# An issue order from a list schedule whose urgencies are shifted by fixed seeds

## The chip, the cores and the metric

The kernel runs on one core of a Trainium2 chip. The metric is device time in microseconds of one execution; the median of several runs counts, and less is better. The engines are called by the profile's short names: PE is TensorE's matmuls and PEld its weight loads, DVE is VectorE, ACT is ScalarE, POOL is GpSimd, SP is SyncE, which issues most transfers.

## The reference

Two branches work on one input of 2048 rows and 512 columns, and a gate mixes them. The first branch builds a convolution kernel of length 2048 for each of the 512 channels from a sum over 128 complex modes, convolves the input with it through Fourier transforms, and adds a skip term. The second is linear attention with 32 heads, whose feature map is a softmax of a small projection and of its negative.

```python
def reference(A_u, A_A_re, A_A_im, ..., B_wqkv, B_w_phi, B_wo, gate_w):
    x = A_u
    g = sigmoid((x * gate_w).sum(-1, keepdims=True))
    # first branch
    logdA = dt * (A_re + 1j * A_im); dB = dt * Bc          # dt = exp(log_dt)
    P = exp(logdA[:, :, None] * l[None, None, :])          # l = 0 .. 2047
    K = einsum("dn,dnl,dn->dl", Cc, P, dB).real
    a = irfft(rfft(pad(u)) * rfft(pad(K)))[..., :L] + u * Dskip
    # second branch, head width 16
    q, k, v = split(x @ wqkv)
    phi(t) = concat(softmax(t @ w_phi), softmax(-(t @ w_phi)))
    b = (phi(q) @ (phi(k).T @ v)) / (phi(q) @ sum(phi(k)) + 1e-6) @ wo
    return g * a + (1 - g) * b
```

## The kernel before

The work is first written down as a plan and only then issued. Each call of `P.add` enters one piece: the engine that does it (or a choice of ACT and DVE for some PSUM evictions), its cost in microseconds, the function that issues its instructions, the pieces that it waits for, and the buffers that it takes and drops. A piece is one to some dozens of instructions. `P.dma` enters a transfer as its issue on SP and its landing. When everything is entered, `Plan.run` puts the pieces into one order, by a list schedule over the plan's own times, and then calls their functions in that order. Each engine thus gets a fixed queue, and on the chip each queue is worked off strictly in order.

The list schedule repeats one step. Of all pieces whose predecessors are placed, and which find their buffer and (on ACT) the right table set, it takes the one that can start earliest in the plan's time. Among pieces with the same start it takes the one with the highest urgency (`n.prio`), which is the sum of costs on the longest chain of pieces behind it, with 0.2 us for each change of engine. A piece that waits for a busy engine starts when the engine comes free, so equal starts are frequent. `boost` adds to the urgency but is set to 0.0 everywhere.

Rings limit the order. `ps` has two PSUM slots that serve every stage; `p0` has two that serve the start, `bk` three for keys and queries, and `pf` two that open when the queries are done. In SBUF, A and R have two buffers each, KD one, Eq (`r8`) two, E and cs four each. A piece that takes a slot waits for the piece that drops it.

The stages, in the order of their entry:

- `prepare`: constants, trigonometric tables, the tables C and D of the modes, the transposed input xT.
- `keys_and_spectrum`: the input's spectrum XU, then the gate, then keys and values for eight pairs of row blocks. The gate is five pieces: 64 small products `gps`, a clip, an exponential, a reciprocal (into `gT`), and a second product `zps` with the eviction into `at.zrow`.
- `queries_and_convolution`, first the queries: four batches, each with four products pq and their exponentials into Eq, a normaliser in steps z1 to z5 (ACT, DVE, ACT, DVE, ACT; the last makes `apm`), and for each of four row blocks two products aexp, two DVE products into Eq, and one block of 12 matmuls into bps (eight with Mw and Eq, four for the skip term). z2 reads `at.zrow`.
- The convolution for eight halves h of 64 channels: `plan_tables` makes E (exponentials) and cs (sines) from `args` products, and switches ACT to the sine tables and back; its two args tiles for the sines hold both PSUM slots that they took until the sines are made. `kgen` makes, for two chunks, A (two halves of three DVE products, L1065 to L1067) and R (L1077 to L1080), then the product kps (64 small matmuls, L241), its eviction KD (L1098), two products psA (L1110) and their evictions XA. `transform` goes on with psB, XK, the spectral products t, psz, a round trip through DRAM (Zd, ZT), psy and the output bS.

The A and R products of the first halves may run during the queries. From half 2 on, the psA products wait for `sq`, the piece that closes the queries, frees their buffers and opens `pf`. Half h + 2's tables are entered after half h's kgen.

Of the kernel before, what the change touches and what calls it, by code (L numbers as in the profile page):

```python
# [91 lines left out]
class Plan:  # L92


    LAT = 0.2

    def __init__(self, rings, psum):
        self.k, self.dyn, self.nodes = dict(rings, **psum), set(psum), []
        self.boost = 0.0
        self.keys, self.shut = {}, {"bk", "pf"}  # L100

    def add(self, eng, cost, fn, deps=(), take=(), drop=(), late=0.0, rw=("", ""), tab=None, sets=None, opens=None):
        n = Bag()
        n.eng, n.cost, n.fn, n.take, n.drop, n.late = eng, cost, fn, list(take), list(drop), late
        n.tab, n.sets, n.opens, n.ring = tab, sets, opens, None
        n.deps = [d for d in deps if d is not None]
        for k in rw[0].split() + rw[1].split():
            wr, rd = self.keys.setdefault(k, (None, []))
            n.deps += ([wr] if wr is not None else []) + (rd if k in rw[1].split() else [])
        for k in rw[0].split():  # L110
            self.keys[k][1].append(n)
        for k in rw[1].split():
            self.keys[k] = (n, [])
        n.users, n.t, n.i, n.boost = [], None, len(self.nodes), self.boost
        n.psum = None
        if "psum" in n.drop:
            n.psum = [d for d in n.deps if d.dyn][0]
        n.dyn = any(not isinstance(r, str) or r in self.dyn for r in n.take)
        for d in n.deps:
            d.users.append(n)  # L120
        self.nodes.append(n)
        return n
# [11 lines left out]
            self.keys[k] = (n, [])  # L134
        return n

    def run(self):
        self.nodes = list(self.nodes)

        for r, k in self.k.items():  # L140
            if r in self.dyn:
                continue
            tk = [n for n in self.nodes for x in n.take if x == r]
            dr = [n for n in self.nodes for x in n.drop if x == r]
            for j, n in enumerate(tk):
                for d in ([dr[j - k]] if j >= k else []) + ([tk[j - 1]] if j and tk[j - 1] is not n else []):
                    assert d.i < n.i
                    n.deps.append(d)
                    d.users.append(n)
        for n in reversed(self.nodes):  # L150
            n.prio = n.boost + n.cost + max([u.prio - u.boost + self.LAT * (u.eng != n.eng) for u in n.users], default=0.0)
        free = {}
        taken = {r: 0 for r in self.k}
        given = {r: {} for r in self.k}
        left = list(self.nodes)
        state, since = None, {}
        order = []
        while left:
            best = None
            for n in left:  # L160
                if any(d.t is None for d in n.deps):
                    continue
                best_e = None
                for e, c in (n.eng if isinstance(n.eng, list) else [(n.eng, n.cost)]):
                    t = free.get(e, 0.0) if e not in "WX" else 0.0
                    for d in n.deps:
                        t = max(t, d.end + (self.LAT if d.at != e else 0.0))
                    if best_e is None or t + c < best_e[0]:
                        best_e = (t + c, t, e, c)
                _, t, e, c = best_e  # L170
                if n.tab is not None and n.tab != state:
                    continue
                ok, ring = True, None
                for r in n.take:
                    if isinstance(r, str) and r not in self.dyn:
                        continue
                    alt = []
                    for q in ([r] if isinstance(r, str) else r):
                        m = taken[q] - self.k[q]
                        if q in self.shut or (m >= 0 and m not in given[q]):  # L180
                            continue
                        alt.append((max(t, given[q][m] + self.LAT if m >= 0 else since.get(q, 0.0)), -self.k[q] + taken[q], q))
# [4 lines left out]
                if not ok:  # L187
                    continue
                key = (t, -n.prio, n.i)
                if best is None or key < best[0]:  # L190
                    best = (key, n, e, c, ring)
            assert best is not None, "no piece can start"
            (t, _, _), n, e, c, ring = best
            n.t, n.end, n.at = t, t + c, e
            free[e] = n.end
            if ring is not None:
                n.ring, n.slot = ring, taken[ring]
                taken[ring] += 1
            if n.psum is not None:
                k = n.psum  # L200
                given[k.ring][k.slot] = n.end
            if n.sets is not None:
                state = n.sets
            if n.opens is not None:
                self.shut.discard(n.opens)
                since[n.opens] = n.end
                self.shut.add({"bk": "p0", "pf": "bk"}[n.opens])
            left.remove(n)
            order.append(n)
        order.sort(key=lambda n: (n.t, n.i))  # L210
        self.order = order
        for n in order:
            self.cur = n
            n.fn()
        return max(n.end for n in order)


def build_selectors(nc, persist, tp, icol):

# [386 lines left out]
def keys_and_spectrum(P, tc, nc, g, psum):  # L606
# [23 lines left out]
    for h in range(2):  # L630
        X = Bag()
        en = []
        for g4 in range(gw // 4):
# [15 lines left out]
            a = P.add("PE", 1.0, pa, [a] if g4 else last, take=[("ps", "p0") if h == 0 else "ps"] + (["XAu"] if g4 == 0 else []), rw=("ud0 ud1 ud2 ud3 W1", ""))  # L649
            en.append(evict(ea, [a]))  # L650
        for r0 in range(0, 32, 4):
# [11 lines left out]
            a = P.add("PE", 0.75, pb, en + [a], take=[("ps", "p0") if h == 0 else "ps"], rw=("TB0 TB1 TB2", ""), drop=(["XAu"] if r0 == 28 else []))  # L663
# [5 lines left out]
    for h in range(2):  # L669
# [15 lines left out]
        a = P.add("PE", 1.2, fa, last + ([a] if h else []), take=["ps"] + ([] if h else ["XAu"]), rw=("wqk ic", ""))  # L685
        fn.append(evict(fe, [a]))
    for h in range(2):
# [16 lines left out]
        a = P.add("PE", 1.2, fb, fn + [a, at_n], take=["ps"], drop=(["XAu"] if h else []))  # L704
# [29 lines left out]
    a = P.add("PE", 1.8, ga, xt + [at_n], take=["ps"])  # L734
    b = P.add("DVE", 0.2, gb, [a], drop=["psum"])
    b = P.add("ACT", 0.2, lambda: act(out=G.z[:], in_=G.z[:], func=ACT.Exp, scale=-1.0), [b, lnexp], tab="L")
    P.add("DVE", 0.4, gc, [b])

    def gd():
        G.ps = psum([128, 4, 128], "zps")  # L740
# [7 lines left out]
        nc.vector.tensor_scalar(out=at.zrow[:], in0=G.ps[:], scalar1=80.0, scalar2=-80.0, op0=ALU.min, op1=ALU.max)  # L748
        G.ps = None
    a = P.add("PE", 1.1, gd, [b, sp], take=["ps"])  # L750
    P.add("DVE", 0.6, ge, [a], drop=["psum"])

    kv = []
    for s2 in range(8):
        K = Bag()
        red = []
        for u in range(2):
# [20 lines left out]
            a = P.add("PE", 1.05, pk, [a] if u else [sp, lnexp] + xt + kp, take=["bk"] + ([] if u else ["Ek", "Zk", "vr"]))  # L778
            x = P.add("ACT", 1.22, ex, [a] + ([x] if u else []), drop=["psum"], tab="L")
# [8 lines left out]
        for u in range(2):  # L788
# [25 lines left out]
            a = P.add("PE", 1.05, pv, [a], take=["bk"], rw=("wqk", ""))  # L814
            c = P.add("DVE", 1.36, sc, [a, l], drop=["psum"])
# [54 lines left out]
def queries_and_convolution(P, tc, nc, g, psum, sh, sp, sl, kv, bank, evict):  # L870
# [36 lines left out]
    a = P.add("PE", 0.9, f2, [n1], take=[psq])  # L907
    n3 = evict(f3, [a])
    mw = []
    for i in range(0, 8, 2):  # L910
# [11 lines left out]
        a = P.add("PE", 0.55, f4, [n3, a], take=[psq])  # L922
# [4 lines left out]
        g.shift_keys()  # L927
    sk = P.add("X", 0.0, shift_k, mw + [sl])

    P.boost = 0.0  # L930
    qdone = []
    for b in range(4):
        Q = Bag()
        eq = []
        for m in range(4):
# [14 lines left out]
            a = P.add("PE", 1.0, pq, [sh, sp] + ([a] if m else []), take=["bk"] + ([] if m else ["r8"]))  # L950
# [35 lines left out]
            act(out=Q.apm[:], in_=Q.lnZ[:], func=ACT.Exp, scale=-1.0)  # L986
            Q.lnZ = Q.den = None
        n = P.add("ACT", 0.8, z1, [z], tab="L")
        n = P.add("DVE", 1.0, z2, [n], drop=["acc"])
        n = P.add("ACT", 0.35, z3, [n], tab="L")  # L990
        n = P.add("DVE", 0.4, z4, [n])
        za = P.add("ACT", 0.35, z5, [n], tab="L")
        pb = None
        for i in range(4):
            j = 4 * b + i
            em = []
            for mp in range(2):
# [12 lines left out]
                a = P.add("PE", 0.3, pe, [za], take=["bk"])  # L1010
# [30 lines left out]
    P.boost = 0.0  # L1041

    xan = [0, 0]

# [261 lines left out]
    T, prev = {}, []  # L1306
# [25 lines left out]
def full_kernel(tc, A_u, A_A_re, A_A_im, A_B_re, A_B_im, A_C_re, A_C_im, A_log_dt, A_Dskip,  # L1332
# [7 lines left out]
    with ExitStack() as ctx:  # L1340
# [181 lines left out]
```

## Time and profile before

| what | value |
|---|---|
| median of 3 runs | 359.31 us (357.62 to 360.52) |
| profiled execution | 359.8 us, its span 358.0 us |
| mean granted TensorE clock | 0.80 of full speed |
| busy share of the span | DVE 79%, PE 71%, ACT 71%, PEld 42%, POOL 3% |
| data moved | 24.62 MB, 69 GB/s over the span |

The profiled execution is one run on the chip; its span goes from the first to the last instruction. A busy share is an average over the whole span, so it says little about any one stage. [...]

### The profile page before, as it was taken

To read this page: it belongs to the slowest core of one execution; us is meant where nothing else is said; L and a number is where in the kernel's file an instruction comes from. 1 tells how busy PE (TensorE), PEld (TensorE's weight loads), DVE (VectorE), ACT (ScalarE), POOL (GpSimd) and SP (SyncE) were. 2 spreads that over 40 slices of the span, in tenths; PEclk is the share of its full clock that TensorE was granted. 3 is DMA by queue.
4 is the path that set the end of the run, shared out by engine and by line. 5 is a ranking of instruction groups with operands and counts; after the bars stand their busy time and mean duration, and the time that the engine had idled before them with its cause. 6 is when DMAs were issued, how large, how long until landed. Compare 5 with 4: busy or idle time off the path is not lost.

```text
span 358.0 us, 9785 instructions
## 1 busy us (share of the span) xinstructions
PE 255.8 (71%) x4291; PEld 150.7 (42%) x4320; DVE 283.8 (79%) x482; ACT 254.7 (71%) x328; POOL 10.3 (3%) x24
## 2 busy tenths in 40 slices
PE   0235684769998895798999769669586847985850
PEld 0234563664444352353455424435244522554640
DVE  8959999986999978999547872169989998697521
ACT  2397999867757689838875692769899897985400
POOL 7200010000000000000000000000000000000000
PEclk9985667657999999598999967757857986585995
DMA  7993400000000000011021001631515264689354
GB/s 202 204 110 75 103 3 0 2 2 0 4 3 2 2 2 2 0 23 37 19 46 31 16 15 29 134 135 55 127 56 122 90 148 146 131 197 207 112 95 66
DMA packets 58665, 24.62 MB, mean 69 GB/s; under 512 B 54144, under 2 KB 55296, under 8 KB 58112
## 3 DMA queue, kind: packets, MB, share of 16 engines
q1 hardware_dynamic: 54400, 23.10, 29.0%
q10 hardware_dynamic: 4224, 0.92, 1.2%
q8 instruction: 33, 0.54, 0.6%
q14 instruction: 8, 0.07, 0.1%
HBM read 11.42 MB, written 8.39 MB: 55 GB/s over the span
## 4 chain that ended last, share of the span: by engine, by line
DVE 42%; PE 33%; ACT 11%; issue 7%; DMA 4%; SPq 1%; DVEq 0%; ACTq 0%
PE bps L1018 7%; DVE A L1065 4%; DVE Atmp L1066 4%; PE pq L943 4%; DVE A L1067 4%; DVE Zk L776 4%; DVE vr L800 3%; PE kps L241 3%; DVE R L1080 2%; PE aexp L1003 2%; ACT cs L83 2%; ACT L75 2%; DMA wqk<-in_B_wqkv_dram 2%; DVE pt L454 2%; DVE R L1079 2%
## 5 line engine op out<-in xcount | busy, mean ns | idle before, releaser
L1018 PE MATMUL bps<-Mw,Eq 128*128 128x512 bf16 x120 | 33.5, 414 | 2.4 <-DVE Eq L1008 1.6
L1008 DVE TENSOR_TENSOR Eq<-Eq,aexp 128x512 bf16<-128x512 bf16 x32 | 20.3, 682 | 17.8 <-PE aexp L1003 17.6
L83 ACT ACTIVATE E<-args 128x1024 bf16<-128x1024 f32 x32 | 31.5, 1030 | 3.2 <-PE args L837 3.2
L1065 DVE TENSOR_TENSOR A<-Ctab,Dtab 128x1024 bf16<-128x1024 bf16 x32 | 21.9, 684 | 13.7 <-PE kps L241 13.6
L837 PE MATMUL args<-selE,stat 64*128 64x512 bf16 x64 | 23.2, 468 | 11.0 <-ACT cs L83 5.3
L83 ACT ACTIVATE cs<-args 128x1024 bf16<-128x1024 f32 x32 | 30.7, 1030 | 0.1
L241 PE MATMUL kps<-R,A 128*32 128x64 bf16 x1024 | 19.5, 236 | 13.2 <-DVE R L1080 5.1
L75 ACT ACT_TABLE_LOAD x20 | 25.7, 1283 | 1.1 <-PEq L1506 0.7
L642 PE MATMUL psA<-W,UD 128*64 128x256 bf16 x128 | 14.9, 398 | 14.8 <-ACT pt L453 6.3
L241 PEld LDWEIGHTS <-A 128*32 128x32 bf16 x1024 | 17.5, 152 | 18.8 <-issue 16.4
L83 ACT ACTIVATE Ek<-pk 128x512 bf16<-128x512 f32 x32 | 16.6, 607 | 9.9 <-PE pk L764 9.9
L1067 DVE TENSOR_TENSOR A<-A,Atmp 128x1024 bf16<-128x1024 bf16 x32 | 22.1, 692 | 1.1
L1079 DVE TENSOR_TENSOR R<-E,cs 128x1024 bf16<-128x1024 bf16 x32 | 21.9, 683 | 0.9 <-ACT cs L83 0.9
L1028 ACT CAST bs<-bps 128x512 bf16<-128x512 f32 x16 | 9.4, 586 | 17.6 <-PE bps L1021 14.3
L1066 DVE TENSOR_TENSOR Atmp<-Ctab,Dtab 128x1024 bf16<-128x1024 bf16 x32 | 21.8, 682 | 0.0
L1207 PE MATMUL psz<-t,TI 128*128 128x512 bf16 x47 | 19.2, 506 | 2.5 <-issue 1.3
L1018 PEld LDWEIGHTS <-Eq 128*128 128x128 bf16 x128 | 12.7, 105 | 19.1 <-issue 6.5
L776 DVE TENSOR_REDUCE Zk<-Ek 128x64 f32<-128x1024 bf16 x16 | 18.7, 1212 | 2.4 <-ACT Ek L83 2.3
L642 PEld LDWEIGHTS <-UD 128*64 128x64 bf16 x128 | 12.8, 206 | 16.9 <-issue 16.5
L800 DVE TENSOR_TENSOR vr<-vp,vr 128x512 bf16<-128x512 f32 x32 | 19.4, 678 | 0.0
L556 PE MATMUL xps<-ident,UD 128*128 128x128 bf16 x64 | 5.8, 249 | 18.4 <-DMA UD<-in_A_u_dram 15.6
L1177 ACT CAST XK<-psB 128x1024 bf16<-128x1024 f32 x16 | 15.9, 1019 | 4.4 <-issue 1.7
(197 smaller groups left out, 578.9 us busy)
## 6 DMA issues: line engine op xcount, KB each, us to landing
XUs<-XU SPq DMA_DIRECT2D x8, 512.0 KB, 5.7
Zd<-Zr SPq DMA_DIRECT2D x14, 256.0 KB, 2.3
ZT<-Zd SPq DMA_DIRECT2D x6, 512.0 KB, 6.0
UD<-in_A_u_dram SPq DMA_DIRECT2D x16, 128.0 KB, 5.1
bSd<-bs SPq DMA_DIRECT2D x16, 128.0 KB, 1.9
bS<-bSd SPq DMA_DIRECT2D x4, 512.0 KB, 7.6
out_dram<-bS SPq DMA_DIRECT2D x30, 64.0 KB, 2.3
wqk<-in_B_wqkv_dram SPq DMA_DIRECT2D x1, 1024.0 KB, 6.9
```

The costliest lines, as they stand in the source:

```text
L75: p = self.nc.scalar.preload_act_table_set(name)
L83: i = self.nc.scalar.activation(**kw)
L241: nc.tensor.matmul(kps[32 * dj:32 * dj + 32, g4, e, :], lhsT=A[:, ri, :, :, d].rearrange("p a b -> p (a b)"), rhs=R[:, ri, d, :], start=(r ...
L642: nc.tensor.matmul(box.ps[64 * e:64 * e + 64, i, :], lhsT=g.UD[:].rearrange("p t (e g) -> p g e t", e=2)[:, gw * h + 4 * g4 + i, e, :], rh ...
L776: nc.vector.tensor_reduce(out=K.Z[:, u, :, :], in_=K.E[:, u, :, :].rearrange("p g (h f) -> p g h f", f=16), axis=mybir.AxisListType.X, op= ...
L800: nc.vector.tensor_tensor(out=K.v[:, u, sg, :, 0:32].rearrange("p m (h e) -> p m h e", e=16), in0=box.ps[:].rearrange("p (m h e) -> p m h ...
L837: nc.tensor.matmul(box.ps[:, 8 * j:8 * j + 8, :], lhsT=g.stat[0:64, G, :], rhs=g.selE[0:64, d0:d0 + 8, :], start=True, stop=True, tile_pos ...
L1018: nc.tensor.matmul(box.ps[:], lhsT=Q.e[:, m, sg, 128 * i:128 * i + 128], rhs=g.Mw[:, 4 * sg + m, :], start=(k == 0), stop=False, skip_grou ...
L1065: nc.vector.tensor_tensor(out=c.A[:, o], in0=Cb(i0), in1=Db(j0), op=ALU.mult)
L1066: nc.vector.tensor_tensor(out=tmp[:], in0=Cb(i1), in1=Db(j1), op=ALU.mult)
L1067: nc.vector.tensor_tensor(out=c.A[:, o], in0=c.A[:, o], in1=tmp[:], op=op)
L1079: nc.vector.tensor_tensor(out=c.R[:, o, :, 32:64], in0=E[:, :, 32:64], in1=x, op=ALU.mult)
```

## The change

Nothing is computed differently. The scheduler is split into `prepare` (ring edges and urgencies), `schedule` (the list schedule, which now gets a shift for each piece and a slack, here 0.0) and `bias` (the shifts). `bias` goes through 50 entries of `TIES`. Each entry is a seed, an amplitude and a share: a generator started with that seed picks that share of the pieces and adds to each a uniform shift between minus and plus the amplitude. The shifts add to the urgency and so decide only between pieces with the same earliest start. The seeds were found by a local search that counted the length of the plan in the plan's own times. Besides, the gate's last two pieces become predecessors: `zrow`'s eviction of z2 in each batch, and both of `sq`. The always-zero `boost` goes.

```diff
     LAT = 0.2
+    SLACK = 0.0
+    TIES = ((52116, 4, 0.1), (24065, 0.5, 0.1), (41416, 1, 0.1), (45222, 1, 0.05), (61293, 2, 0.02), (71070, 0.5, 0.1),
...
+            (24195, 2, 0.02), (71220, 0.5, 0.05))
...
-            n.prio = n.boost + n.cost + max([u.prio - u.boost + self.LAT * (u.eng != n.eng) for u in n.users], default=0.0)
...
+            n.prio = n.cost + max([u.prio + self.LAT * (u.eng != n.eng) for u in n.users], default=0.0)
+
+    def schedule(self, bias, slack=0.0):
...
+                if ok:
+                    cand.append((t, -n.prio - bias[n.i], n.i, n, e, c, ring))
+            if not cand:
+                return None, None
+            lim = min(cand)[0] + slack
+            t, _, _, n, e, c, ring = min(cand, key=lambda x: (max(x[0], lim), x[1], x[2]))
...
+    def bias(self, seeds):
+        import random
+        b = [0.0] * len(self.nodes)
+        for s, amp, share in seeds:
+            r = random.Random(s)
+            for i in range(len(b)):
+                if r.random() < share:
+                    b[i] += r.uniform(-amp, amp)
+        return b
+
+    def run(self):
+        self.tail = {}
+        self.prepare()
+        T, order = self.schedule(self.bias(self.TIES), self.SLACK)
...
-    P.add("DVE", 0.4, gc, [b])
+    g.gate = [P.add("DVE", 0.4, gc, [b])]
...
-    P.add("DVE", 0.6, ge, [a], drop=["psum"])
+    g.gate.append(P.add("DVE", 0.6, ge, [a], drop=["psum"]))
...
-        n = P.add("DVE", 1.0, z2, [n], drop=["acc"])
+        n = P.add("DVE", 1.0, z2, [n, g.gate[1]], drop=["acc"])
...
-    sq = P.add("X", 0.0, shift_q, qdone + [n for n in P.nodes if n.psum is not None and "bk" in n.psum.take], opens="pf")
...
+    sq = P.add("X", 0.0, shift_q, qdone + g.gate + [n for n in P.nodes if n.psum is not None and "bk" in n.psum.take], opens="pf")
```

## Rows read from the trace of the kernel before

**Rows 1.** The page: busy us, share of the span, instructions of each engine.

```profile
PE 255.8 (71%) x4291; PEld 150.7 (42%) x4320; DVE 283.8 (79%) x482; ACT 254.7 (71%) x328; POOL 10.3 (3%) x24
```

**Rows 2.** Busy us (instructions) of PE, PEld, DVE, ACT, POOL; PE clock, DMA share, GB/s.

```profile
140.00:232.00 92.00, 76.60 (x815) 37.50 (x825) 62.83 (x112) 62.89 (x88) 0.00 (x0) 0.85 0.15 32
232.00:322.00 90.00, 66.95 (x1344) 37.30 (x1346) 80.22 (x132) 78.91 (x81) 0.00 (x0) 0.73 0.47 122
```

**Rows 3.** Timeline of DVE, 196 to 242 us: start, us, engine, work, [idle before, releaser].

```profile
220.62 2.48 DVE L1008 TENSOR_TENSOR Eq<-Eq,aexp 128x512 bf16<-128x512 bf16 x4 [6.74 <-PE aexp L1003]
...
231.62 0.69 DVE L1065 TENSOR_TENSOR A<-Ctab,Dtab 128x1024 bf16<-128x1024 bf16 x1 [8.52 <-PE kps L241]
...
238.19 0.69 DVE L1065 TENSOR_TENSOR A<-Ctab,Dtab 128x1024 bf16<-128x1024 bf16 x1 [3.35 <-PE kps L241]
```

**Rows 4.** The same timeline, ACT and DVE: the last query batch's normaliser and the tables.

```profile
202.35 1.28 ACT L75 ACT_TABLE_LOAD   x1
...
203.35 0.41 DVE L983 TENSOR_TENSOR lnZ<-lnZ,den 128x256 f32<-128x256 f32 x1
...
207.93 1.28 ACT L75 ACT_TABLE_LOAD   x1
...
209.22 0.42 ACT L83 ACTIVATE apm<-lnZ 128x256 bf16<-128x256 f32 x1
```

**Rows 5.** The same timeline, PE and ACT: half 1's and half 2's K generation.

```profile
197.29 1.01 ACT L1098 CAST KD<-kps 128x1024 bf16<-128x1024 f32 x1 [1.08 <-PE kps L241]
...
220.74 0.61 PE L1110 MATMUL psA<-W,KD 128*128 128x256 bf16 x4
...
226.36 0.60 PE L855 MATMUL args<-selE,stat 64*128 64x512 bf16 x2
...
228.41 3.77 ACT L83 ACTIVATE cs<-args 128x1024 bf16<-128x1024 f32 x4
...
230.40 1.17 PE L241 MATMUL kps<-R,A 128*32 128x64 bf16 x64 [3.43 <-ACT cs L83]
...
237.45 0.68 PE L241 MATMUL kps<-R,A 128*32 128x64 bf16 x31 [3.41 <-issue]
```

**Rows 6.** Groups by line: the three A products; busy us, mean ns.

```profile
L1065 DVE TENSOR_TENSOR A<-Ctab,Dtab 128x1024 bf16<-128x1024 bf16 x32 | 21.9, 684 | 13.7 <-PE kps L241 13.6
...
L1066 DVE TENSOR_TENSOR Atmp<-Ctab,Dtab 128x1024 bf16<-128x1024 bf16 x32 | 21.8, 682 | 0.0
...
L1067 DVE TENSOR_TENSOR A<-A,Atmp 128x1024 bf16<-128x1024 bf16 x32 | 22.1, 692 | 1.1
```

**Rows 7.** Busy us in four-us windows (as in rows 2), 200 to 212 us.

```profile
200.00:204.00 4.00, 2.37 (x16) 0.94 (x14) 3.69 (x8) 2.62 (x4) 0.00 (x0) 1.00 0.15 33
204.00:208.00 4.00, 1.64 (x11) 0.80 (x10) 3.30 (x6) 3.98 (x6) 0.00 (x0) 1.00 0.15 33
208.00:212.00 4.00, 3.08 (x14) 1.15 (x13) 3.97 (x8) 3.75 (x5) 0.00 (x0) 0.52 0.00 0
```

**Rows 8.** Timeline of PE, 140 to 197 us: two blocks of eight bps matmuls.

```profile
159.11 1.89 PE L1018 MATMUL bps<-Mw,Eq 128*128 128x512 bf16 x8
...
164.61 3.16 PE L1018 MATMUL bps<-Mw,Eq 128*128 128x512 bf16 x8
```

**Rows 9.** Timelines of PE and ACT, 64 to 140 us: the gate and the spectrum.

```profile
71.10 1.81 PE L724 MATMUL gps<-gw,xT 128*128 128x1 bf16 x64 [0.41 <-DVE XAu L621]
...
73.92 1.01 ACT L623 CAST XU<-psB 128x1024 bf16<-128x1024 f32 x1 [2.18 <-PE psB L254]
...
100.93 1.05 PE L743 MATMUL zps<-xT,gwr 128*32 128x512 bf16 x16
```

**Rows 10.** Timeline of DVE, 290 to 358 us: two waits of the tail.

```profile
306.44 1.23 DVE L1291 TENSOR_TENSOR bS<-psy,gT 128x1024 bf16<-128x1024 f32 x1 [3.26 <-PE psy L1270]
...
334.36 0.69 DVE L1184 TENSOR_TENSOR t<-XU,XK 128x1024 bf16<-128x1024 bf16 x1 [3.83 <-ACT XK L1177]
```

**Rows 11.** The page's DMA queues: packets, MB, share of 16 engines.

```profile
q8 instruction: 33, 0.54, 0.6%
```

More of the change, by code (lines that the diff above doesn't have):

```diff
@@ L150, in run @@
         for n in reversed(self.nodes):
-            n.prio = n.boost + n.cost + max([u.prio - u.boost + self.LAT * (u.eng != n.eng) for u in n.users], default=0.0)
-        free = {}
-        taken = {r: 0 for r in self.k}
+            n.prio = n.cost + max([u.prio + self.LAT * (u.eng != n.eng) for u in n.users], default=0.0)
+    def schedule(self, bias, slack=0.0):
+        free, taken = {}, {r: 0 for r in self.k}
         given = {r: {} for r in self.k}
-        left = list(self.nodes)
-        state, since = None, {}
-        order = []
+        shut, state, since, order = set(self.shut), None, {}, []
+        for n in self.nodes:
+            n.t, n.ring, n.open, n.ready = None, None, len(n.deps), 0.0
+        left = [n for n in self.nodes if not n.open]
         while left:
-            best = None
+            cand = []
             for n in left:
-                if any(d.t is None for d in n.deps):
-                    continue
                 best_e = None
@@ L186, in run @@
                     t, _, ring = min(alt)
[L187 to L193, printed above, removed]
-            n.t, n.end, n.at = t, t + c, e
-            free[e] = n.end
-            if ring is not None:
+                if ok:
[4 more added lines that the diff above has]
+            t, _, _, n, e, c, ring = min(cand, key=lambda x: (max(x[0], lim), x[1], x[2]))
+            n.t, n.end, n.at = t, t + c, e
+            n.before = [(d, self.LAT if d.at != e else 0.0) for d in n.deps]
+            if e in free and e not in "WX":
+                n.before.append((self.tail[e], 0.0))
+            if e not in "WX":
+                free[e] = n.end
+                self.tail[e] = n
+            if ring is not None:
+                m = taken[ring] - self.k[ring]
+                if m >= 0:
+                    n.before.append((given[ring][m], self.LAT))
+                elif ring in since:
+                    n.before.append((since[ring], 0.0))
                 n.ring, n.slot = ring, taken[ring]
@@ L204, in run @@
             if n.opens is not None:
-                self.shut.discard(n.opens)
-                since[n.opens] = n.end
-                self.shut.add({"bk": "p0", "pf": "bk"}[n.opens])
+                shut.discard(n.opens)
+                since[n.opens] = n
+                shut.add({"bk": "p0", "pf": "bk"}[n.opens])
+            n.c = c
             left.remove(n)
+            for u in n.users:
+                u.open -= 1
+                if not u.open:
+                    left.append(u)
             order.append(n)
         order.sort(key=lambda n: (n.t, n.i))
-        self.order = order
+        return max(n.end for n in order), order
+    def bias(self, seeds):
[11 more added lines that the diff above has]
+        T, order = self.schedule(self.bias(self.TIES), self.SLACK)
+        assert order is not None, "no piece can start"
         for n in order:
@@ L214, in run @@
             n.fn()
-        return max(n.end for n in order)
+        return T
 def build_selectors(nc, persist, tp, icol):
```

19 lines of the change are left out of this document (8 added, 11 removed), and 7 rows, old and new, of the table TIES.

## The prediction

> **What bounds the kernel now.** I read the busy line first: VectorE is busy 79% of the span, TensorE and ScalarE 71% each [rows 1]. No engine is full over the whole span, so the next view is the busy time by stage [rows 2]. From 232 to 322 us, the convolution, VectorE works 80.2 of 90 us and ScalarE 78.9: both are nearly full, and an order can win little there by itself. From 140 to 232 us, the queries, VectorE works 62.8 of 92 us, ScalarE 62.9 and TensorE 76.6: here 29 us of VectorE lie idle although the next stage is short of exactly that engine. That is the place to look at, because kernel generation (the A and R products) belongs to no stage: it may run as soon as its rings have room. What follows 322 us ends in a chain of single steps.
>
> The third view is the timeline of 196 to 242 us, where the idle time has names. VectorE waits 6.74 us before an Eq product at 220.62, 8.52 us before an A product at 231.62, and 3.35 us before the next at 238.19 [rows 3]. Two causes stand behind them. First, the last query batch: its normaliser is ready when VectorE ends lnZ at 203.76 (203.35 + 0.41), but ScalarE had loaded the sine tables at 202.35, came back to the exponential tables with the load at 207.93, and made apm only at 209.22: 5.46 us later [rows 4]. TensorE, whose aexp and bps work needs apm, is busy only 2.37, 1.64 and 3.08 of the three 4 us from 200 to 212, so 4.9 us idle [rows 7]. Second, the K generation of half 2: the KD of half 1 was evicted at 197.29, its second psA product (which frees the one KD buffer) came at 220.74, and the two PSUM slots of ring `ps` then went to args tiles of the next tables, the second at 226.36. They come free only as ScalarE works through four sines from 228.41; the first kps product waited 3.43 us for that and ran at 230.40. Only then were the two A buffers free again, and VectorE went on at 231.62 [rows 3, 5].
>
> **The change part by part.** No instruction is removed or added: the pieces, their code and their costs are the same. Four things differ.
>
> *The refactored scheduler.* The candidates, their start times and the ring checks are the same; with SLACK at 0 the limit is the earliest start, so a piece that can start earlier still goes first and urgency still decides only among equal starts. The removed boost was 0 everywhere. Cost and gain nothing; what hides nothing needs no cover here, since planning is done before the launch.
>
> *The gate edges.* Before, the last pieces of the gate had no users, so their urgency was nearly their own cost; now z2 of each batch and the opening of `pf` wait for them. Both were long done when they are needed (the gate's 64 small matmuls ran at 71.10, the product behind zrow at 100.93 [rows 9], the z2 pieces come in the stage from 140 us), so the wait costs 0; if it were met, everything behind z2 on VectorE's queue, A, R and Eq products, would stand with it. But their urgency becomes that of the query chain: they will be placed sooner. In the trace they stand between the spectrum's products: 1.81 us on TensorE, and the first XU eviction behind them found ScalarE idle for 2.18 us [rows 9]. The bounds are 0 and 2.18 us of gain; if they move into another busy place they cost the same 1.81. I take +0.7, less than half, since VectorE had work during most of that wait.
>
> *The shifted urgencies.* Fifty seeds, each touching 2 to 10% of the pieces by up to 0.5 to 8 us: by the sum of share x amplitude squared / 3 a piece is shifted by some 1.9 us (one standard deviation), and 87% of the pieces get a shift of some size. Against urgencies that span the whole plan this is small: the stages stay, neighbours change places. So the gain has to come from orders that differ by a few pieces, and the two causes above are of that kind.
>
> (a) If apm of the last batch (0.42 us) goes ahead of the sine tables, the rest of the query stage starts up to 5.46 us earlier; TensorE can use 4.9 us of that, the idle it now has [rows 4, 7]. Below: 0, or a loss of about 1.8 us if the table switch that is put off then holds R (its two sines take 1.94). Value: 3.5, nearer to the 4.9 because TensorE is the engine that the rest of this stage waits for: 76.6 of 92.
>
> (b) If half 1's psA and half 2's kps go ahead of the args tiles, two more A chunks fit into the idle 15.26 us (6.74 + 8.52). A chunk is two halves of three products: 2 x (684 + 682 + 692) ns = 4.12 us [rows 6], so two are 8.23 us that leave the full stage behind. What is late next is ScalarE: it has 11.1 us idle in 232 to 322 [rows 2], and R of half 3 needs the sines that now run from 228.41. Bounds 0 and 8.23; I take 5.0, somewhat above the middle, because only half of the two chunks must find a place in idle time that is nearly twice as long.
>
> (c) In the tail the wait of 3.26 us before bS at 306.44 and of 3.83 us before t at 334.36 are order as well: psy queued behind args, XK behind other evictions [rows 10]. Bounds 0 and 7.1; I take 1.0, since the steps after 336 us are a chain that no order shortens.
>
> *What is lost.* The plan knows neither TensorE's clock nor stalls for which the profile shows no cause. One block of kps matmuls is split by 3.41 us of "issue" [rows 5]. An order fitted to the plan's own times has less slack against these. I take -1.5, between 0 and the one stall of 3.41 us. These gaps fit a refill of the instruction stream: 33 packets of instructions [rows 11] stand against 8611 TensorE instructions [rows 1], one per 261. [...]
>
> Sum: 0.7 + 3.5 + 5.0 + 1.0 - 1.5 = 8.7 us. The profiled execution took 359.8 us, 358.0 of span and 1.8 around it, 0.5 above the median of 359.31; so 359.8 - 8.7 = 351.1, and against the median 350.6. I give 350.8.
>
> **The rivals.** *More is gained*: both causes go fully, 4.9 + 8.2, with the tail's 1.0 and the front's 0.7: 14.8 us, 344.5. For it: idle time is there, and order is all that was searched. Against: ScalarE is left with little in the next stage, and a shift decides only between equal starts.
>
> *Nothing that counts*: the searched order is shorter in its plan only. The plan's fractions of a us are smeared on the chip by the 3.41 us stall and by matmuls whose time the plan has wrong: eight bps matmuls took 1.89 us in one place and 3.16 in another [rows 8]. Also the case in which the shifts flip pairs with no effect on the two causes. For it: the differences that the shifts make are of about 2 us, the size of these errors. It gives 356 to 362, say 358.5.
>
> *Slower*: the new order spreads TensorE's work in the query stage, and its clock falls. [...] The price is that of a bps block, 3.16 - 1.89 = 1.27 us, and there are 16 [rows 8]. If the stage were granted 0.73, as the next one is, its 76.6 us of TensorE would be 76.6 x 0.85 / 0.73 = 89.2; with half of today's 15.4 us of idle left that makes 96.9 instead of 92, +4.9, so 364.2. It decides from the clock at which work and that half idle fill 92 us: 76.6 x 0.85 / 84.3 = 0.77. Against it: the search shortens this very stage, which packs TensorE more densely. [...]
>
> **How the numbers follow.** Forecast (350.8, some 347 to 355): 0.42. More gained: 0.15. Nothing that counts: 0.26. Slower: 0.17. The runs before differ by 0.8% (357.62 to 360.52), so about 1% is what can be told from no change: 355.7 and 362.9 are the borders. Faster is the first two, 0.57; within 1% 0.26; slower 0.17. The range leaves out the upper half of the slow case and a little below the best one: 343.5 to 362.5.
>
> **What would show it.** In the profile after: VectorE's idle from 140 us to the opening of the convolution falls from 29 to some 20 us; apm of the fourth batch comes within 1 us of its lnZ; kps of half 2 stands before the last bps; the convolution's first loads, of XUs and bS, are issued some 4 us earlier than now; the gate's 64 matmuls stand before 71 us. I am wrong if those idle pieces reappear elsewhere under other names, if ScalarE's idle in the convolution stage grows as VectorE's shrinks, or if the granted clock of the query stage falls below 0.77.

## The result, and the profile after

The changed kernel takes 339.1 us (median; 337.52 to 341.89) against 359.4 before; the ratio is 0.9448 (95% interval 0.9369 to 0.9528). By this ratio it is 19.8 us less, between 17.0 and 22.7; differences are taken from such ratios throughout. The forecast was 350.8 with a range of 343.5 to 362.5: the direction was right, the size less than half.

The busy line of the page after, in the form of [rows 1]:

```profile
PE 249.9 (73%) x4320; PEld 145.7 (43%) x4320; DVE 279.3 (82%) x478; ACT 257.2 (76%) x332; POOL 12.2 (4%) x24
```

VectorE does 4.5 us less work than before: on balance four evictions that may go to either engine went to ScalarE (482 instructions have become 478). That was not in the prediction; it is work ahead of 140 us, where the new order gains nothing (the last kvp product ended at 128.4 us before and ends at 129.5 now).

The stages, as in [rows 2] (busy us of PE, PEld, DVE, ACT, POOL; clock, DMA share, GB/s):

```profile
140.00:232.00 92.00, 80.63 (x1005) 40.45 (x1005) 74.44 (x132) 74.65 (x101) 0.00 (x0) 0.93 0.19 47
232.00:322.00 90.00, 68.21 (x1724) 41.98 (x1727) 80.99 (x130) 76.27 (x79) 0.00 (x0) 0.83 0.56 138
```

From 140 to 232 us VectorE works 74.4 of 92 us and no longer 62.8. A part of this is convolution, which now begins earlier: up to its first loads (issued at 227.58 before, at 221.25 after) VectorE lay idle for 25.2 us from 140 us before and for 17.5 after. To see where the time was saved, four moments serve: the last eviction of a bps block (the end of the queries), the KD evictions of half 2 and of half 7, and the end. The first fence is of the kernel before, from ScalarE's timeline; the second, of several engines, of the kernel after.

```profile
205.47 0.59 ACT L1028 CAST bs<-bps 128x512 bf16<-128x512 f32 x1
...
218.16 0.58 ACT L1028 CAST bs<-bps 128x512 bf16<-128x512 f32 x1 [2.98 <-PE bps L1021]
...
226.51 0.58 ACT L1028 CAST bs<-bps 128x512 bf16<-128x512 f32 x1 [1.36 <-PE bps L1021]
...
238.19 1.01 ACT L1098 CAST KD<-kps 128x1024 bf16<-128x1024 f32 x1 [2.77 <-PE kps L241]
```

```profile
200.21 1.28 ACT L75 ACT_TABLE_LOAD   x1
...
207.09 0.42 ACT L83 ACTIVATE apm<-lnZ 128x256 bf16<-128x256 f32 x1 [0.58 <-DVE lnZ L1021]
...
207.41 0.57 ACT L1066 CAST bs<-bps 128x512 bf16<-128x512 f32 x1
...
209.20 0.61 PE L1147 MATMUL psA<-W,KD 128*128 128x256 bf16 x4
...
211.60 1.89 PE L1056 MATMUL bps<-Mw,Eq 128*128 128x512 bf16 x8
...
211.84 0.58 ACT L1066 CAST bs<-bps 128x512 bf16<-128x512 f32 x1 [0.94 <-ACT XA L1153]
...
214.40 1.28 ACT L75 ACT_TABLE_LOAD   x1
...
219.65 2.10 PE L280 MATMUL kps<-R,A 128*32 128x64 bf16 x128
...
220.16 0.61 ACT L1066 CAST bs<-bps 128x512 bf16<-128x512 f32 x1
220.78 1.28 ACT L75 ACT_TABLE_LOAD   x1
220.93 0.69 DVE L1116 TENSOR_TENSOR R<-E,cs 128x1024 bf16<-128x1024 bf16 x1 [4.38 <-PE kps L280]
...
222.07 1.01 ACT L1135 CAST KD<-kps 128x1024 bf16<-128x1024 f32 x1
```

Before, 12.7 us pass between the twelfth bps eviction (205.47) and the thirteenth (218.16); after, 4.4 (207.41 to 211.84). Before, half 2's KD comes 11.7 us behind the last bps eviction; after, 1.9. The sine switch of half 2, which stood between lnZ and apm of the last batch [rows 4], is over at 200.21 + 1.28, ahead of that batch's normaliser, and the one of half 3, at 227.11 before, is at 214.40. The two kps blocks run without a break at 219.65; the gap of 3.41 us [rows 5] is gone. VectorE's wait of 8.52 us [rows 3] has become 4.38. Half 1's second psA product, at 220.74 before [rows 5], is at 209.20.

In the table, us from the start of the profiled execution. Each row is one execution, and that of the change was the longest of its four (341.89 us), so its differences are a little small.

| kernel | last bps eviction | half 2's KD | half 7's KD | span |
|---|---|---|---|---|
| before | 226.5 | 238.2 | 326.0 | 358.0 |
| after | 220.2 | 222.1 | 307.2 | 340.1 |
| difference | -6.4 | -16.1 | -18.8 | -17.9 |

So 6.4 us are won at the end of the queries, 9.8 between that and half 2's KD, 2.7 in the convolution, and 0.9 are lost in the tail; executions of the change differ by 4.4 us among themselves, so the small terms are readings of these two traces and no more. Why so little in the convolution is in the windows from half 2's to half 7's KD, first before, then after:

```profile
238.20:326.00 87.80, 65.49 (x1288) 36.09 (x1295) 81.26 (x134) 76.54 (x79) 0.00 (x0) 0.73 0.47 117
```

```profile
222.10:307.20 85.10, 61.47 (x1371) 34.98 (x1371) 83.36 (x137) 77.92 (x80) 0.00 (x0) 0.86 0.58 146
307.20:340.10 32.90, 18.65 (x728) 13.58 (x722) 11.10 (x14) 8.72 (x9) 0.00 (x0) 0.71 0.53 109
```

VectorE works 81.3 of 87.8 us there before and 83.4 of 85.1 after, 98%: the stage is full. TensorE's granted clock there was 0.73 before and 0.86 after; no run separates that from the order.

### The profile page after: what moved, and what is told of

Read it like the earlier page. It is cut to its first block, busy times and chain, and to the rows that moved or that the text cites. A ratio compares the mean times of both kernels' runs of the same rounds, so it can differ in the third digit from the quotient of the medians.

```text
span 340.1 us, 9815 instructions
## 1 busy us (share of the span) xinstructions
PE 249.9 (73%) x4320; PEld 145.7 (43%) x4320; DVE 279.3 (82%) x478; ACT 257.2 (76%) x332; POOL 12.2 (4%) x24
## 4 chain that ended last, share of the span: by engine, by line
DVE 40%; PE 37%; ACT 7%; issue 6%; DMA 4%; SPq 3%; ACTq 1%; DVEq 0%
PE bps L1056 7%; DVE R L1117 5%; DVE A L1104 5%; DVE Atmp L1103 5%; DVE A L1102 5%; PE pk L803 5%; PE vp L835 4%; PE pq L981 3%; PE args L876 3%; SPq L1428 3%; DVE R L1116 3%; DMA Cim<-in_A_C_im_dram 2%; PE kps L280 2%; PE aexp L1041 2%; PE psz L1276 2%
## 5 line engine op out<-in xcount | busy, mean ns | idle before, releaser
L1056 PE MATMUL bps<-Mw,Eq 128*128 128x512 bf16 x128 | 31.9, 394 | 1.1 <-DVE Eq L1046 1.1
L1046 DVE TENSOR_TENSOR Eq<-Eq,aexp 128x512 bf16<-128x512 bf16 x32 | 20.4, 682 | 10.2 <-PE aexp L1041 10.2
L681 PE MATMUL psA<-W,UD 128*64 128x256 bf16 x128 | 15.6, 396 | 16.8 <-DMA ldc<-in_A_log_dt_dram 5.7
L1116 DVE TENSOR_TENSOR R<-E,cs 128x1024 bf16<-128x1024 bf16 x32 | 21.9, 685 | 4.4 <-PE kps L280 4.4
L876 PE MATMUL args<-selE,stat 64*128 64x512 bf16 x64 | 21.3, 446 | 5.1 <-ACT cs L83 2.9
L815 DVE TENSOR_REDUCE Zk<-Ek 128x64 f32<-128x1024 bf16 x16 | 18.8, 1214 | 6.0 <-ACT Ek L83 5.8
L1104 DVE TENSOR_TENSOR A<-A,Atmp 128x1024 bf16<-128x1024 bf16 x32 | 22.1, 692 | 1.1
L1102 DVE TENSOR_TENSOR A<-Ctab,Dtab 128x1024 bf16<-128x1024 bf16 x32 | 21.9, 685 | 1.2 <-PE kps L280 1.2
L1103 DVE TENSOR_TENSOR Atmp<-Ctab,Dtab 128x1024 bf16<-128x1024 bf16 x32 | 21.9, 684 | 0.0
L595 PE MATMUL xps<-ident,UD 128*128 128x128 bf16 x64 | 7.5, 296 | 18.9 <-DVE tgv L397 10.4
L1244 PE MATMUL psz<-t,TI 128*128 128x512 bf16 x56 | 18.2, 457 | 4.2 <-ACT cs L83 3.0
L681 PEld LDWEIGHTS <-UD 128*64 128x64 bf16 x128 | 12.2, 205 | 20.1 <-issue 19.8
L83 ACT ACTIVATE Eq<-pq 128x512 bf16<-128x512 f32 x32 | 16.8, 614 | 3.3 <-PE pq L981 3.3
L1056 PEld LDWEIGHTS <-Eq 128*128 128x128 bf16 x128 | 12.0, 101 | 16.9 <-DVE Eq L1046 3.0
L1214 ACT CAST XK<-psB 128x1024 bf16<-128x1024 f32 x16 | 16.1, 1027 | 1.5 <-PE psB L1206 1.0
```

The lines of the kernel that those rows point to most:

```text
L83: i = self.nc.scalar.activation(**kw)
L681: nc.tensor.matmul(box.ps[64 * e:64 * e + 64, i, :], lhsT=g.UD[:].rearrange("p t (e g) -> p g e t", e=2)[:, gw * h + 4 * g4 + i, e, :], rh ...
L876: nc.tensor.matmul(box.ps[:, 8 * j:8 * j + 8, :], lhsT=g.stat[0:64, G, :], rhs=g.selE[0:64, d0:d0 + 8, :], start=True, stop=True, tile_pos ...
L1046: nc.vector.tensor_tensor(out=e, in0=e, in1=box.ps[:], op=ALU.mult)
L1056: nc.tensor.matmul(box.ps[:], lhsT=Q.e[:, m, sg, 128 * i:128 * i + 128], rhs=g.Mw[:, 4 * sg + m, :], start=(k == 0), stop=False, skip_grou ...
L1102: nc.vector.tensor_tensor(out=c.A[:, o], in0=Cb(i0), in1=Db(j0), op=ALU.mult)
```

## The experiments

Three theories stood against each other. Theory 1: the list schedule's plan tells the time; whatever makes the plan shorter by so much does the same on the chip. Theory 2: only a part arrives, or it comes from something else (the gate's edges, the two spots of the prediction). Theory 3: what matters is the state in which the queries are left, marked by half 2's KD, because the convolution behind it is full. "Plan" is the length of the schedule by the plan's own costs: 379.5 us for the kernel before, 359.5 for the change. Each kernel is the changed one with the edit shown; e9 and e10 have no shifts either (as e1), so they stand on the order of before. Differences are (ratio - 1) x 359.4 us.

**e1, e2, e3, e4: other shifts.** The whole edit of each is its list of seeds:

```diff
+    TIES = ()                                              # e1
+    TIES = ((17791, 4, 0.02),)                             # e2
+    TIES = ((52116, 4, 0.1), ..., (37415, 2, 0.05))        # e3: the first 25 of the fifty
+    TIES = ((39173, 2, 0.02),)                             # e4
```

> All fifty shifts are taken out; the refactored scheduler and the gate's new predecessors stay. The plan is then 379.5 us long, as that of the kernel before. Theory 1 (the plan's differences carry over to the chip one for one): no change, 359.4 us, 358 to 361. Theory 2 (a part of the gain is the gate's edges): 357 or less, with the gate's 64 matmuls ahead of 71 us.

> One single other seed, amplitude 4 on 2% of the pieces, in place of the fifty; the plan is 369.9 us, 9.6 shorter than before. Theory 1 (differences carry over one for one): 349.8 us. Theory 2 (only the fitted order's two spots count, other differences of the plan are smeared on the chip by clock and stalls; half or less of a difference arrives): 354.6 or more.

> Only the first 25 of the fifty seeds; the plan is 364.2 us, 15.3 shorter than before and 4.7 longer than the full change. Theory 1: 344.0 us. Theory 2 (half arrives): 351.7 us or more.

> One single seed, amplitude 2 on 2% of the pieces, picked because its plan is long: 401.4 us, 21.9 longer than before. Theory 1 (the plan tells the chip's time in both directions): 381.3 us. Theory 2 (the chip's engines run on past what the plan takes for a wait; half or less arrives): 370 us or less.

| kernel | plan against before | ratio (interval) | measured difference |
|---|---|---|---|
| e1 | 0.0 | 1.0026 (0.9985 to 1.0067) | +0.9 |
| e2 | -9.6 | 0.9636 (0.9557 to 0.9715) | -13.1 |
| e3 | -15.3 | 0.9525 (0.9473 to 0.9577) | -17.1 |
| the change | -20.0 | 0.9448 (0.9369 to 0.9528) | -19.8 |
| e4 | +21.9 | 1.0185 (1.0117 to 1.0254) | +6.6 |

e1 is no change: the edges do nothing; without shifts every engine's queue is that of before, piece by piece, and the gate's matmuls stand at 72.7 us, with the change even later. Theory 2 falls for the three shorter plans: all of the difference arrives, in e2 some more (10.2 to 15.9 us for 9.6). For the longer plan of e4 less than a third does. e2 also shows that an earlier end of the queries is not needed: its last bps eviction is at 228.8 us, 2.3 later than before, but half 2's KD is at 226.2 and the span 346.1.

**e5, e6, e7: shifts on the late pieces alone, or on the early ones alone.** A shift counts only for pieces whose number lies in a range; 747 is the first piece behind half 3's kgen. e5 has the fifty seeds on the pieces before 747; e6 and e7 have one seed each, (62141, 8, 0.1) and (92661, 2, 0.1), on the pieces from 747 on.

```diff
-        for s, amp, share in seeds:
+        for s, amp, share, lo, hi in seeds:
...
-                    b[i] += r.uniform(-amp, amp)
+                    x = r.uniform(-amp, amp)
+                    b[i] += x if lo <= i < hi else 0.0
```

> The fifty seeds as in the change, but shifting only the pieces entered up to half 3's K generation; the later pieces keep their plain urgencies. Up to half 2's KD the order is that of the change. The plan is 363.9 us, 4.4 longer than that of the change. Theory 1 (every difference of the plan carries over): 343.5 us. Theory 3 (from half 2's KD on the convolution is at the limit of its engines, some 118 to 120 us whatever the order, and only the moment of that KD counts): 339 to 341 us.

> The order of before up to half 3's K generation, one seed (amplitude 8, 10%) for the later pieces only, picked for a long plan: 391.6 us, 12.0 longer than before. Theory 1: 371.5 us. Theory 3: 359 to 362 us.

> The order of before up to half 3's K generation, one seed (amplitude 2, 10%) for the later pieces only, picked for a short plan: 373.4 us, 6.2 shorter than before. Theory 1: 353.3 us. Theory 3: 357.5 to 360 us.

Measured: e5 0.9479 (0.9434 to 0.9525), 1.1 us above the change where its plan is 4.4 above; e6 1.0126 (1.0066 to 1.0187), +4.5 us for a plan of +12.0; e7 0.9983 (0.9951 to 1.0014), -0.6 for -6.2. So of the plan's differences behind half 3's K 10 to 38% arrives. The differences of e5 and e7 are within the noise. e5 keeps 18.7 of the 19.8 us: nearly the whole gain hangs on the order of the early pieces. Theory 3 has these three better than theory 1, though e6 lies 1.9 us above its range.

**e9 and e14: the sine switch in the last query batch.** e9 adds one edge to the order of before, so that half 2's switch comes behind apm; e14 adds the opposite edge to the change, so that it falls between z3 and z5 again.

```diff
-    b = P.add("ACT", 1.28, lambda: act.begin(TRIG), T.nE + [a for a, _ in ra] + prev, sets="T", tab="L")
+    b = P.add("ACT", 1.28, lambda: act.begin(TRIG), T.nE + [a for a, _ in ra] + prev + ([P.apm] if h == 2 else []), sets="T", tab="L")   # e9; in e14 P.z3 for P.apm
```

> No shifts; the order of before with one added edge: half 2's switch to the sine tables waits for apm of the last query batch. The order up to that point is that of before. If the 5.5 us that apm waits for the tables are what holds the last batch (step a of the prediction): the gap between the twelfth and the thirteenth bps eviction falls from 12.7 us to 5 to 8, the last bps eviction comes 5 to 8 us earlier against kernels with the order of before, and the time is 352 to 356 us if the rest follows. If the end of the queries is not what the convolution waits for: that eviction is earlier, but half 2's KD and the end move by less than 2 us, 357 us or more.

> The change with one edge added: half 2's switch to the sine tables waits for the step before the last of the last query batch's normaliser (z3), so that it falls between z3 and z5 again, as in the kernel before. Up to there the order is that of the change; the plan is 365.3 us, 5.8 longer. Step a of the prediction, at the size that the opposite edit showed (7 us): 344 to 347 us, with a gap of 9 us or more between the twelfth and thirteenth bps eviction. If the switch is hidden in the denser order: below 341.5 us.

e9 measured 0.9800 (0.9732 to 0.9868), -7.2 us; e14 0.9576 (0.9522 to 0.9630), 4.6 us more than the change, where its plan is 5.8 longer. ScalarE's timeline of e9, then of e14:

```profile
206.59 0.42 ACT L83 ACTIVATE apm<-lnZ 128x256 bf16<-128x256 f32 x1 [1.46 <-DVE lnZ L1013]
207.03 1.28 ACT L75 ACT_TABLE_LOAD   x1
...
210.15 0.59 ACT L1059 CAST bs<-bps 128x512 bf16<-128x512 f32 x1
...
213.90 0.59 ACT L1059 CAST bs<-bps 128x512 bf16<-128x512 f32 x1
```

```profile
202.29 1.28 ACT L75 ACT_TABLE_LOAD   x1
...
205.41 0.59 ACT L1059 CAST bs<-bps 128x512 bf16<-128x512 f32 x1
...
209.16 0.42 ACT L83 ACTIVATE apm<-lnZ 128x256 bf16<-128x256 f32 x1
218.10 0.59 ACT L1059 CAST bs<-bps 128x512 bf16<-128x512 f32 x1 [2.98 <-PE bps L1052]
...
227.47 0.63 ACT L1059 CAST bs<-bps 128x512 bf16<-128x512 f32 x1
```

With the switch back inside, the gap of before is there again to the tenth: 205.41 to 218.10, 12.7 us; in e9 it is 3.75. In e14 the last bps eviction is 7.3 us later than in the change, and so is half 2's KD (229.4 against 222.1). As a time, step a is shown in both directions, at 7.2 and 4.6 us.

In e9 one expectation failed. Against e1, which has the order of before, the last bps eviction comes only 2.8 us earlier (225.3 against 228.1) and not 5 to 8. Of the shorter gap 3.1 us come from its early end: the twelfth eviction now waits behind the switch (210.15 against 207.10). Half 2's KD is 4.8 us earlier (235.0 against 239.9) and half 7's 7.3 (320.3 against 327.6), so more than half of the 7.2 us shows behind the queries; why it does was not isolated.

The windows from 200 to 220 us show slow time beside the idle time; before, after and e14:

```profile
200.00:220.00 20.00, 14.88 (x64) 5.78 (x63) 11.84 (x22) 13.65 (x16) 0.00 (x0) 0.74 0.08 17
```

```profile
200.00:220.00 20.00, 18.69 (x134) 8.72 (x137) 11.98 (x23) 16.26 (x22) 0.00 (x0) 1.00 0.18 40
```

```profile
200.00:220.00 20.00, 15.74 (x69) 6.29 (x67) 10.82 (x20) 13.73 (x17) 0.00 (x0) 0.74 0.09 20
```

TensorE's granted clock was 0.74 and is 1.00; with the switch inside it is 0.74 again. Before, TensorE worked 1.64 of the 4 us from 204 [rows 7], and from 208 to 218 its clock was 0.50 to 0.52. In these three rows the clock is higher where more work was done (18.69 us at 1.00, against 14.88 and 15.74 at 0.74), but e9's row, below, has 0.91 at 15.45 us: what sets the clock is not shown. Two rows of the kernel before, both at a clock of 0.50, give the price:

```profile
210.63 1.03 PE L1110 MATMUL psA<-W,KD 128*128 128x256 bf16 x4
...
214.89 2.77 PE L1018 MATMUL bps<-Mw,Eq 128*128 128x512 bf16 x6 [0.22 <-issue]
```

In the change, at 1.00, four psA matmuls take 0.61 us and eight of bps 1.89. So these two rows alone carry some 1.8 us of slow time (an estimate: 1.03 - 0.61, and 2.77 less six eighths of 1.89), beside the 4.9 us idle. In e9 the clock of the window is 0.91:

```profile
200.00:220.00 20.00, 15.45 (x127) 7.69 (x118) 15.55 (x28) 13.62 (x18) 0.00 (x0) 0.91 0.09 20
```

**e8b: the sine switch of half 3.** The order of the change is kept; the pieces of one list are taken out of it and put back behind the last bps block: the last two bps evictions, half 3's second tile of sine args, its switch, its sine pieces and the switch back.

```diff
+        held = self.mark[-2:] + self.held
+        order = [n for n in order if n not in held]
+        k = order.index(self.last) + 1
+        order[k:k] = held
...
+    if h == 3:
+        P.held = [ra[1][0], b] + T.nc + [T.end]
```

> The order of the change with one thing undone: the second sine args tile of half 3, the switch to the sine tables, the four sines and the switch back stand behind the last bps block and its eviction, as in the kernel before; nothing else is moved. If the early sine switch is what brings half 2's KD from 11.7 us behind the last bps eviction (before) to 1.9 us (the change): the KD comes about 8 us behind that eviction and the time is 346 to 349 us. If that gap was the 3.4 us stall and chance, or if the convolution swallows it: 342 us or less.

Measured 0.9524 (0.9469 to 0.9579), 2.7 us above the change: between the two expectations, and not clear of the noise of the two kernels. The timeline shows the wait itself as expected: 7.0 us from the last bps eviction to KD, not 1.9.

```profile
219.33 0.59 ACT L1064 CAST bs<-bps 128x512 bf16<-128x512 f32 x1 [1.36 <-PE bps L1057]
219.94 1.28 ACT L75 ACT_TABLE_LOAD   x1
221.23 3.77 ACT L83 ACTIVATE cs<-args 128x1024 bf16<-128x1024 f32 x4
...
226.32 1.01 ACT L1134 CAST KD<-kps 128x1024 bf16<-128x1024 f32 x1
```

In the profiled executions KD is 4.3 us later than in the change and the span 3.5 longer: most of the wait reaches the end.

**e10: the stall in half 2's kps.** TensorE waits there for nothing that the profile shows ("issue"). It was 3.41 us before, and 3.96, 3.50, 3.37 and 2.94 in e1, e6, e7 and e9, which share the early order (e9 but for the switch), always 31 matmuls ahead of the block's end; no kernel with the change's early order has it there.

```diff
+        order = [n for n in order if n not in self.held]
+        k = order.index(self.kds[2]) + 1
+        order[k:k] = self.held
...
-                nc.sync.dma_start(out=L.XUs[64 * i:64 * i + 64], in_=XU[64 - 64 * i:128 - 64 * i, Q])
+                (nc.sync if Q else nc.scalar).dma_start(out=L.XUs[64 * i:64 * i + 64], in_=XU[64 - 64 * i:128 - 64 * i, Q])
...
+        if Q == 0:
+            P.held = [L.nx.issue, L.nb.issue]
```

> No shifts; the order of before, but the convolution's first loads (XUs and bS of the first quarter, 1 MB) are issued from ScalarE's queue behind half 2's KD eviction, and no longer at the end of the queries. If the 3.4 to 4.0 us stall in half 2's kps, which every kernel with this early order shows, is TensorE's instruction refill behind these loads: the block runs without a gap over 1 us, KD comes at most 9 us behind the last bps eviction instead of 11.7, and the time is 0 to 3 us less (the loads may be awaited then). If the stall belongs to the place in the instruction stream whatever the transfers do: the gap stays at 3 us or more and the time is not less.

Here `kds[2]` is half 2's KD eviction; bS is issued from ScalarE's queue in the same way. Measured 0.9988 (0.9951 to 1.0025), no difference. From e1's timeline of TensorE, then from e10's of TensorE and VectorE:

```profile
239.12 0.68 PE L272 MATMUL kps<-R,A 128*32 128x64 bf16 x31 [3.96 <-issue]
```

```profile
236.25 0.69 PE L275 MATMUL kps<-R,A 128*32 128x64 bf16 x31 [0.75 <-issue]
```

```profile
244.54 0.69 DVE L1220 TENSOR_TENSOR t<-XUs,XK 128x1024 bf16<-128x1024 bf16 x1 [2.99 <-DMA XUs<-XU]
```

The stall shrinks from 3.96 to 0.75 us, at the same matmul, and KD comes 9.0 us behind the last bps eviction (237.0 against 228.0) and no longer 11.7. The DMA share from 233 to 236 us, ahead of the matmul, was 1.01 in e1 and is 0.13. So the stall is long where these loads run ahead of it; that their issue also went to another queue was not separated. The time that is won is given back at once: VectorE waits 2.99 us for XUs, and half 3's KD comes at 255.3, against 255.0 in e1.

Such a stall does not belong to the old order alone. In e12, below, one of nearly 4 us stands in half 6's kps, 24 matmuls ahead of the block's end, behind a DMA share of 1.08 (276 to 280 us):

```profile
283.87 0.58 PE L283 MATMUL kps<-R,A 128*32 128x64 bf16 x24 [3.94 <-issue]
```

**e11, e12, e13: further searches.** In all three some TensorE pieces are priced nearer to the trace (those of the diff, and two whose price goes by their size), and the seeds were searched again with these prices.

```diff
+    COSTS = {'zz': 1.2, 'kp': 1.15, 'fi': 1.0, 'iz': 2.6, 'pbm': 2.05, 'pk': 0.95, 'pv': 0.95, 'pq': 0.95, 'kn': 0.42}   # e11, e13
+    COSTS = {'zz': 1.4, 'kp': 1.2, 'fi': 1.2, 'iz': 2.7, 'pbm': 2.05, 'pk': 0.98, 'pv': 0.98, 'pq': 0.98}               # e12
```

> An order found by a further search that brings half 2's KD forward: with some TensorE pieces re-priced from the trace (the zs block 1.2 instead of 2.4 us, kps 1.15, psz 1.0 and the like) that KD stands at 212.9 us of the plan, against 236.2 for the change's order at the same prices, while the whole plan is 355.2 us, against 352.1. Theory 1 (the plan's length tells the time): 342 us. Theory 3 in its strong form (the moment of half 2's KD sets the end, some 118 us later): KD near 200 us and 316 to 322 us. Theory 3 in its weak form (it is only a mark of how much of VectorE's work lies behind): KD is early, the distance from it to the end grows by about as much.

> 64 seeds found by a search with re-priced TensorE pieces (zs 1.4 instead of 2.4 us, kps 1.2, psz 1.2 and the like); the plan is 348.1 us, the change's order at these prices 351.0. Theory 1: 336 us. If the change has used up what order can give (VectorE works 98% of the time between half 2's and half 7's KD): 338 to 341 us.

> Many more seeds, from a longer search with prices still closer to the trace; the plan is 349.3 us, the change's order at these prices 352.1, and half 2's KD stands 5.5 us earlier. Theory 1: 336.3 us. Theory 3, strong form: 333 to 335 us. If order is used up: 338 to 341 us.

Measured: e11 0.9400 (0.9339 to 0.9460); e12 0.9205 (0.9146 to 0.9264); e13 0.9254 (0.9206 to 0.9302). Against the change these are -1.7, -8.7 and -7.0 us, the first within the noise, where the plans at their own prices say +3.1, -2.9 and -2.8. So theory 1 misses all three: one sign, and two sizes by a factor of two to three. In e11 half 2's KD is at 199.8 us, 22 earlier than in the change, and the span is 337.9: the strong form of theory 3 falls. From that KD to half 7's pass 105.9 us with VectorE busy 90.4 of them, as the window shows:

```profile
199.80:305.70 105.90, 80.10 (x1522) 44.09 (x1532) 90.38 (x149) 90.72 (x96) 0.00 (x0) 0.86 0.51 130
```

That KD was a mark only as long as nothing else was left behind. e12 is the fastest kernel of the case, below the change by 8.7 us where its plan is 2.9 shorter; order was not used up. Its window from half 2's to half 7's KD, and the one from 200 to 220 us:

```profile
209.60:297.80 88.20, 65.05 (x1390) 38.05 (x1400) 84.02 (x138) 78.90 (x83) 0.00 (x0) 0.81 0.57 146
```

```profile
200.00:220.00 20.00, 18.08 (x271) 10.38 (x272) 15.99 (x27) 16.34 (x20) 0.00 (x0) 0.94 0.37 81
```

The convolution takes 88.2 us, not less than in the change; its KD of half 2 comes 12.5 us earlier, and VectorE works 16.0 of the 20 us from 200, against 12.0 (half of that window lies behind the KD). The gain lies ahead of that KD once more.

## Why the prediction was wrong

The stage was right (VectorE's idle time in the queries, 29 us before) and so was the sign. The sizes were not, and one mechanism was another. Of the signs that I named, VectorE's idle time from 140 to 232 us fell from 29.2 to 17.6, apm comes right behind its lnZ (206.64 + 0.42, then 207.09), and the first loads are issued 6.3 us earlier; but half 2's kps still stands behind the last bps block, and the gate's products came later.

*The refactored scheduler and the gate's edges.* The first was priced right at nothing. The gate was priced at +0.7 and is 0 (e1): the edges alone move no piece, and in the change the 64 matmuls moved from 71.10 [rows 9] to 74.89, not forward.

```profile
74.89 1.83 PE L763 MATMUL gps<-gw,xT 128*128 128x1 bf16 x64 [0.70 <-ACT XAu L662]
```

*Step a, the last batch.* The mechanism was right; the size was too small. I took 3.5 us and bounded it by TensorE's idle 4.9. It measures 7.2 added to the order of before (4.7 to 9.6) and 4.6 taken from the change. The first is above the bound, the second within it. I had counted idle time and not the slow time beside it: the clock in that stretch went from 0.74 to 1.00. I had the clock only as a risk, in the slower rival, which let it fall from 0.85 to 0.73 [rows 2] as TensorE's work is spread; no run shows that spreading is what lowers it, and in this stage it rose to 0.93. That the clock makes the excess is argued from the rows; no run isolates it.

*Step b, half 2's K.* The size was 5.0, and 9.8 us were won there by the profile, but not by my mechanism. Half 1's psA did go ahead, yet half 2's kps stayed behind the last bps block, and no A chunk moved. By the windows up to the first loads for the third A product of a half (L1067 before, L1104 after), before (227.6) and after (221.2), each order has 12 A halves done:

```profile
0.00:227.60 227.60, 8.30 (x12) 0.84 0.19 37
```

```profile
0.00:221.20 221.20, 8.30 (x12) 0.85 0.21 38
```

What moved was half 3's sine switch, 2.7 us of time by e8b (5.1 of the 9.8 us of wait), and the stall of 3.4 us went. I had read kps as held by PSUM slots, which it was, but drawn the profit on the wrong engine.

*The tail*: +1.0 expected, 0.9 lost by the profile from half 7's KD on.

*What is lost*: -1.5 expected. No loss shows: 20.0 us were planned and 19.8 measured, and the change's trace has no TensorE wait above 1.5 us that is marked "issue". That the stall went is not shown to be a gain either: without it the old order was no shorter (e10), and in other orders it comes back at another place (e12).

*The step that failed as a whole* is the sum. It let nearly all of the gain come from two places, and took 3.5 of 4.9 and 5.0 of 8.2 us there. The discount is not all of it: with both places in full I had 344.5 us (chance 0.15), still 5.4 above the measured time. In its place the runs show that step a is worth 4.6 to 7.2 us, that the A chunks of step b did not move, and that the wait between the last bps eviction and half 2's KD, where the sum had no term for half 3's sine switch, fell by 9.8 us.

The plan had the whole: -20.0 planned, -19.8 measured. That it agrees so closely is in part luck, for e2 brought 13.1 for 9.6. Longer plans cost 30 and 38% of what they say in e4 and e6, but 79% in e14; late differences arrive to 10 to 38% (e5 to e7); and with other prices the plan is off by more (e11 to e13).

Open: a and half 3's switch make 7 to 10 of the 19.8 us, the late order 1.1. The rest, 9 to 11 us if the parts add, was not isolated. e14 narrows the place: without step a its queries end as in e1 (last bps eviction at 227.5 and 228.1), but half 2's KD stands at 229.4 against 239.9. So what is left without step a, half 3's switch among it, shows behind the end of the queries, most of it in that wait. Nor was it tried which of the plan's prices makes the long plans too long.

## What to carry to other kernels

When an order is searched over its own time model, test the model on differences: one or two orders with much longer and shorter plans tell how much arrives before any place is priced by hand. It is a test for that search alone: here the shorter plans of the first search arrived whole, those with other prices did not. Price an idle stretch of TensorE with the clock that its work then runs at, not by its idle time alone (here 0.74 against 1.00 in the 20 us from 200; argued, not isolated). In a full stage (VectorE at 93 to 98% here) order won little (2.7 of 87.8 us); look ahead of it for what could have been done there.

## What the runs showed of the hardware

TensorE stalled 2.9 to 4.0 us in the middle of a block of 64 matmuls, at the same instruction in five kernels. In the kernel before, the convolution's first loads were in flight then: the DMA share was 0.93 from 233 to 236 us. With these loads (1.5 MB by e10's list of transfers, three of 512 KB; its expectation has 1 MB) issued at 237.00 and later, the stall was 0.75 us at the same instruction. In e12 a stall of 3.94 us stood in another block, behind a DMA share of 1.08. The prediction and e10 took the stall for a refill of TensorE's instructions, one of 33 packets [rows 11]; that was an estimate from the counts, and no run shows that it is one.
